# Step 0's ScalarE order, both copies of its transposed rows on VectorE, and an earlier k load in a planned attention-and-FFN kernel

## Chip, core and metric

The kernel runs on one core of a Trainium2 chip. Times are device microseconds of that core, the median of several executions. The profile is one execution taken by the hardware profiler; times in it count from the start of its span.

## What is computed

A gated linear attention over 768 positions feeds a gated feed-forward layer (ReGLU). Cut to what matters:

```python
# q, k, v, f_logit: (4, 8, 768, 48); w_gate, w_val: (384, 1536); w_out: (1536, 384)
f = 1.0 / (1.0 + np.exp(-f_logit))
for t in range(S):
    state = f[:, :, t, :, None] * state + np.einsum('bhd,bhe->bhde', k[:, :, t], v[:, :, t])
    y[:, :, t] = np.einsum('bhd,bhde->bhe', q[:, :, t], state)
x = y.transpose(0, 2, 1, 3).reshape(B * S, H * D)       # 3072 tokens x 384
out = (np.maximum(x @ w_gate, 0.0) * (x @ w_val)) @ w_out
```

## The kernel before

Time is cut into six steps (c = 0 to 5) of 128 positions, and each step works on the four batch entries as two pairs (pair 0 is b = 0, 1; pair 1 is b = 2, 3). A tile of one batch entry is 128 positions by 384 columns, 8 heads of 48.

For each pair, ScalarE forms exp(-f) (L563 in step 0, L649 in the others) and its log(1 + x) (L564, L651). TensorE sums that over the positions with a triangular matrix (`cum`, L572 or L658). ScalarE takes the exponentials of plus and minus the sum (L576 and L579 in step 0, L668 and L670 later), and k and q are multiplied by them into `hats` (L582, L584; L680, L683 on GpSimd). TensorE transposes `hats` (L609, L694), the result is copied out of PSUM into `qkT`, and then come the scores (L724), the mask (`ptm`, L734, VectorE), the weighted sum (`intra`, L759), the copy into `xT` (L788, ScalarE) and the state update (L810, L543, L547, L549). Small exponentials of the total decay go into `dec` (L598 in step 0, two per pair).

Step 0 differs from the other steps: `attention_pair` handles two batch entries at once, with two neighbouring positions in one partition. The copy of the transposed k (x = 1) is on VectorE (L617), and that of the transposed q (x = 0) on ScalarE (L616). An entry `tails["first q"]` makes the log of pair 1 (L564) come behind the q copy of pair 0 in ScalarE's order.

The feed-forward layer for the 512 tokens of a step has 12 hidden slices j of 128 (`ffn_hidden`): gate matmuls and value matmuls (L834), a ReLU on ScalarE (L840), a product on VectorE (L844); then the output matmuls (`ffn_out`, L877), a copy (L887) and a store (L891). In steps 0 to 2 the slices 0 to 5 are done for each pair apart, and slices 6 to 11 for all four together. All feed-forward matmuls form one fixed chain: gate 0, value 0, gate 1, and so on. The weights come in three slices each (`wg0` to `wg2`, `wv0` to `wv2`, `wo0` to `wo2`; slice 0 serves j = 0 to 3, slice 1 j = 4 to 7). They are issued by GpSimd, which also converts them to bf16 (L493). The inputs f, k, q, v are loaded by SyncE, one transfer per pair (L473, named f0.0, f0.1, f1.0 and so on: step, pair).

No order is written out by hand apart from the first loads. A class `Plan` takes every operation with a planned duration (`occ`), a latency and a priority, plays the schedule through, and so fixes the order of every engine, SyncE and GpSimd included. Each engine then runs its list strictly in that order and waits on semaphores where needed. `follows` adds an order without a wait; `after` adds a wait. The first loads are given by the string `first`; an item `x@y` is issued only when y has landed:

```python
first = ("f0.0 k0.0 q0.0 v0.0 f0.1 k0.1 q0.1 v0.1 wg0@f0.1 wv0 wg1@q0.1 wv1 wg2 wv2 f1.0@wv1 k1.0 q1.0 v1.0 wo0@q1.0 wo1 wo2 "
         "f1.1 k1.1 q1.1 v1.1").split()
```

The loads of SyncE keep the order of this list among themselves, and the weight transfers of GpSimd likewise. Up to about 15 us, TensorE's planned gaps are filled with matmuls on zeros (L938), which keep it busy and compute nothing.

Of the kernel before, what the change touches and what calls it, by code (L numbers as in the profile page):

```python
# [6 lines left out]
ALU = mybir.AluOpType  # L7
# [292 lines left out]
def bass_hgrn2_outer__then__ffn_reglu_kernel(  # L300
# [13 lines left out]
    x_way = {(c, pr): "tiled" if c < 3 else "xbar" for c in range(6) for pr in range(2)}  # L314
    s_twin = {(c, pr) for c in range(6) for pr in range(2)} - {(0, 0), (1, 0)}
    y_twin = {(1, 1), (2, 0), (2, 1)}
    flight = 3
    wsteps = 3
    first = ("f0.0 k0.0 q0.0 v0.0 f0.1 k0.1 q0.1 v0.1 wg0@f0.1 wv0 wg1@q0.1 wv1 wg2 wv2 f1.0@wv1 k1.0 q1.0 v1.0 wo0@q1.0 wo1 wo2 "
             "f1.1 k1.1 q1.1 v1.1").split()  # L320
    B, H, S, D = q.shape
    C = 128
    NC = S // C
# [66 lines left out]
    def act_t(n):  # L390
        return dict(occ=0.17 + n / 1150.0, lat=0.2)
# [63 lines left out]
    def slot_of(n, c, pr):  # L455
        return (2 * c + pr) % NL[n]

    def in_keys(n, c, b0, b1):
        return [f"{n}{slot_of(n, c, b // 2)}_{b % 2}" for b in range(b0, b1)]

    def load(n, c, b0, b1, after=()):
        last = tails.get("load")
        t = ld[n]
        both = c in twos and n != "v"
        if both:
            src = bass.AP(tensor=srcs[n].tensor, offset=b0 * H * S * D + c * C * D,
                          ap=[[2 * D, C // 2], [S * D, 2 * H], [1, 2 * D]])
            dst = bass.AP(tensor=t, offset=slot_of(n, c, b0 // 2) * 2 * HD, ap=[[NL[n] * 2 * HD, 128], [2 * D, H], [1, 2 * D]])
        else:
            src = bass.AP(tensor=srcs[n].tensor, offset=b0 * H * S * D + c * C * D,  # L470
                          ap=[[D, C], [S * D, (b1 - b0) * H], [1, D]])
            dst = t[:, slot_of(n, c, b0 // 2), :, :, :].rearrange("p b h d -> p (b h) d")
        op = add("SP", lambda: sy.dma_start(dst, src), [], in_keys(n, c, b0, b1),  # L473
                 occ=0.7 if both else 1.0, lat=0.9, prio=c * 100, after=after,
                 follows=[last] if last else [])
        tails["load"] = op
        dma(op, f"{n}{slot_of(n, c, b0 // 2)}", 0.95 * (b1 - b0), (64, 19, 27) if both else (128, 13.5, 23))
        return op

    WJ = NJ // wsteps  # L480
# [15 lines left out]
        dma(op, f"{nm}{s}", 2.45, (32, 62, 80, 2.2) if nm == "wo" else (24, 80, 80, 2.9))  # L496
        return op

    loads, done = [], {}
    for item in first:  # L500
        item, _, behind = item.partition("@")
        gate = [done[behind]] if behind else []
        if item[0] == "w":
            op = load_w(item[:2], int(item[2:]), gate)
        else:
            c, pr = (int(x) for x in item[1:].split("."))
            op = load(item[0], c, 2 * pr, 2 * pr + 2, gate)
        done[item] = op
        if item[0] != "w":
            loads.append(op)  # L510

# [40 lines left out]
    def attention_pair(c, b0):  # L552
# [9 lines left out]
        bkeys = [f"bn{bi}_0", f"bn{bi}_1"]  # L562
        add("ACT", lambda: sc.activation(raw["f"], raw["f"], AF.Exp, scale=-1.0), key["f"], key["f"], prio=P, **act_t(2 * HD))  # L563
        add("ACT", lambda: sc.activation(bn[:, :, :, 0:D], by_i["f"], AF.Ln, bias=1.0), key["f"] + [f"bneg{bi}"], bkeys, prio=P,  # L564
            follows=tails.pop("first q", []), **act_t(2 * HD))
        heads = lambda b_: b_.ap[:, 0:HD].rearrange("p (h d) -> p h d", h=H)
        for i in range(2):
            bc, ek = Bank("bc4"), Bank("bc4")

            def cum(i=i, bc=bc):  # L570
                for o in range(2):
                    mm = te.matmul(bc.ap[:, 0:HD], (upto if o <= i else below)[:, :], bn[:, o, :, 0:D], start=(o == 0), stop=(o == 1))  # L572
                return mm
            chain("cum", "PE", cum, ["upto", "below", f"bneg{bi}"] + bkeys, [bc], occ=0.33, lat=PE_L, prio=P + 1, opens=[bc])
            ex = expo[:, e0 + i, 0, :]
            add("ACT", lambda bc=bc, ek=ek: sc.activation(ek.ap[:, 0:HD], bc.ap[:, 0:HD], AF.Exp, scale=1.0),  # L576
                [bc], [ek], prio=P + 2 + i, opens=[ek], **act_t(HD))
            eqk = bc if i else f"expq{e0}_0"
            add("ACT", lambda bc=bc, i=i, ex=ex: sc.activation(bc.ap[:, 0:HD] if i else ex, bc.ap[:, 0:HD], AF.Exp, scale=-1.0),  # L579
                [bc], [eqk], prio=P + 2 + i, **act_t(HD))  # L580
            e, hi = ("DVE" if i else "POOL"), his[i]
            hk_op = add("DVE", lambda i=i, hi=hi, ek=ek: ve.tensor_tensor(hats[:, hi, 1, :, 0:D], by_i["k"][:, i], heads(ek), ALU.mult),  # L582
                        key["k"] + [ek, f"hats{hi}"], hk_(hi), prio=P + 2 + i, **dve_t(HD))
            add(e, lambda e=e, i=i, hi=hi, bc=bc, ex=ex: engine[e].tensor_tensor(  # L584
                hats[:, hi, 0, :, 0:D], by_i["q"][:, i], heads(bc) if i else ex.rearrange("p (h d) -> p h d", h=H), ALU.mult),
                key["q"] + [eqk, f"hats{hi}"], hq_(hi), prio=P + 3 + i, follows=[hk_op] if i else [], **elem_t(e, HD))
# [9 lines left out]
        for j in range(2):  # L596
            lo = 64 * j
            add("ACT", lambda lo=lo, j=j: sc.activation(  # L598
                dec[ai][lo:lo + 64, b0:b0 + 2, :, j].rearrange("p b n -> p n b"),
                tot.ap[lo:lo + 64, 0:2 * NP].rearrange("p (n b) -> p n b", n=NP), AF.Exp, scale=-1.0),  # L600
                [tot, f"dec{ai}"], [f"dec{ai}_{b}{j}{hh}" for b in (b0, b0 + 1) for hh in range(2)], prio=P + 10, **act_t(8))
        for x in (1, 0):
            tp = Bank("tp")

            def transposes(x=x, tp=tp):
# [6 lines left out]
            chain("transposes", "PE", transposes, ["ident"] + [t for hi in his for t in (hk_(hi) if x else hq_(hi))], [tp],  # L612
                  occ=0.5, lat=PE_L, prio=P + 4, opens=[tp])
            dst = bass.AP(tensor=qkT, offset=q0 * 2 * NP * C + x * 2 * NP * C, ap=[[NQ * 2 * NP * C, 128], [1, 2 * NP * C]])
            e = "DVE" if x else "ACT"
            op = add(e, (lambda tp=tp, dst=dst: sc.activation(dst, tp.ap[:, :].bitcast(BF16), AF.Copy)) if e == "ACT"  # L616
                else (lambda tp=tp, dst=dst: ve.tensor_copy(dst, tp.ap[:, :].bitcast(BF16))),  # L617
                [tp], [f"qkT{q0 + b}_{x}{hh}" for b in range(2) for hh in range(2)], prio=P + 4,
                occ=1.02 if e == "ACT" else 0.7, lat=0.2)
            if not x and b0 == 0:  # L620
                tails["first q"] = [op]

    def attention_back(c, b, behind):
        w = c * B + b
# [14 lines left out]
    def attention_front(c, b):  # L639
# [32 lines left out]
        if c < NC - 1:  # L672
            for j in range(2):
# [6 lines left out]
        add("POOL", lambda: gp.tensor_tensor(hk, kin[:, b % 2, :, :], ex[:, 1, :].rearrange("p (h d) -> p h d", h=H),  # L680
                                             ALU.mult),
            in_keys("k", c, b, b + 1) + [f"expk{ei}", f"hats{hi}"], hk_(hi), prio=P + 2, **pool_t(HD))
        add("POOL", lambda: gp.tensor_tensor(hq, qin[:, b % 2, :, :], ex[:, 0, :].rearrange("p (h d) -> p h d", h=H),  # L683
                                             ALU.mult),
            in_keys("q", c, b, b + 1) + [f"expq{ei // 2 * 2}_{ei % 2}", f"hats{hi}"], hq_(hi), prio=P + 2, **pool_t(HD))

        if (c, b // 2) in pe_hats:
            tp = Bank("tp")
# [203 lines left out]
                     occ=0.35 * len(both), lat=0.9, prio=P)  # L892
            dma(op, f"osb{oi}", 0.6, (8, 66, 66), len(both))

    groups = {c: [(0, 2, range(0, n)), (2, 4, range(0, n)), (0, 4, range(n, NJ))] for c, n in halves.items()}
    pend = []
    for c in range(NC):
        for b in range(0, B, 2):
# [32 lines left out]
    for e in pl.ENGINES:  # L931
        pl.free0[e] = 0.8
    spare = banks[-1]
    order = pl.settle([(bk, warm_until if bk is spare else 0.0) for bk in banks], rounds=8, early=set(done.values()))
    waits = pl.needs()

    def warm():
# [91 lines left out]
```

## Time and profile before

| | |
|---|---|
| median of 5 runs | 196.06 us (193.85 to 198.23) |
| the profiled execution | 198.23 us; its span 196.5 us |
| TensorE busy, with the filling matmuls | 185.4 us (94% of the span) |
| ScalarE, VectorE, GpSimd busy | 110.9, 106.2, 75.9 us |
| granted TensorE clock | 1.000 |
| moved by DMA | 31.74 MB, 162 GB/s over the span |

PE is TensorE's matmuls, PEld its weight loads, DVE VectorE, ACT ScalarE, POOL GpSimd, SPq and POOLq the queues of SyncE and GpSimd. A row of the timeline has the start, the length, the engine, the line, the operation with what it writes and reads, and in brackets how long the engine had been idle and what ended that. A row of the table of stretches has the stretch, its length, and the busy time of each engine in it.

### The profile page before, as it was taken

What the parts mean: (1) busy time and instruction counts of PE and PEld (TensorE: products, weight loads), DVE (VectorE), ACT (ScalarE), POOL (GpSimd) and SP (SyncE); (2) the same over time, 40 slices, a digit from 0 to 9 for tenths busy, and PEclk for the clock granted to TensorE, in tenths of its full rate; (3) what the DMA queues carried; (4) which work ended last, traced back from release to release, by engine and by line L of the source; (5) the groups of instructions that cost most, each with busy time, mean ns of one, the idle gap of its engine ahead of it and who ended that gap; (6) DMA issues with size and microseconds to landing.
All of it is one profiled execution on the core that took longest, in us unless ns stands there. A gap on an engine that the chain in (4) does not pass through costs nothing.

```text
span 196.5 us, 4465 instructions
## 1 busy us (share of the span) xinstructions
PE 185.4 (94%) x1790; PEld 110.6 (56%) x1790; DVE 106.2 (54%) x195; ACT 110.9 (56%) x250; POOL 75.9 (39%) x108
## 2 busy tenths in 40 slices
PE   6976899998999999999979979999999999999995
PEld 1445594455778556767744635554554555544564
DVE  7756884771577888354756733742554633442300
ACT  3676449662496879828656757378344433344312
POOL 8367003956375949772623183543230000000000
PEclk9999999999999999999999999999999999999999
DMA  5999999998998999999788897997974110111113
GB/s 136 275 277 206 206 188 214 195 204 170 233 243 176 223 185 178 229 180 232 161 178 151 169 232 148 243 220 160 213 91 99 60 48 16 40 40 43 40 40 120
DMA packets 118196, 31.74 MB, mean 162 GB/s; under 512 B 111136, under 2 KB 118176, under 8 KB 118176
## 3 DMA queue, kind: packets, MB, share of 16 engines
q1 hardware_dynamic: 114192, 27.93, 68.5%
q0 software_dynamic: 3984, 3.54, 11.3%
q8 instruction: 14, 0.23, 0.5%
q14 instruction: 6, 0.05, 0.1%
HBM read 25.95 MB, written 4.72 MB: 156 GB/s over the span
## 4 chain that ended last, share of the span: by engine, by line
PE 64%; DMA 13%; issue 8%; POOL 7%; SPq 5%; ACT 2%; POOLq 0%
PE ps L834 33%; PE ps L877 21%; DMA wo<-in_moe_w_out_dram 5%; SPq L473 4%; DMA k_in<-in_k_dram 3%; DMA q_in<-in_q_dram 3%; DMA f_in<-in_f_logit_dram 3%; PE ps L724 2%; POOL hats L680 2%; POOL hats L683 1%; PE ps L694 1%; PE ps L759 1%; PE ps L658 1%; SPq L795 1%; PE ps L810 1%
## 5 line engine op out<-in xcount | busy, mean ns | idle before, releaser
L844 DVE TENSOR_TENSOR gT<-relu,ps 128x512 bf16<-128x512 bf16 (+1 forms) x90 | 51.3, 578 | 54.0 <-PE ps L834 38.8
L834 PE MATMUL ps<-xT,wv 128*128 128x512 bf16 (+1 forms) x270 | 61.5, 337 | 1.5 <-DMA wv<-in_moe_w_val_dram 1.5
L834 PE MATMUL ps<-xT,wg 128*128 128x512 bf16 (+1 forms) x270 | 61.5, 337 | 0.2 <-ACT relu L840 0.2
L840 ACT ACTIVATE relu<-ps 128x512 bf16<-128x512 f32 (+1 forms) x90 | 45.3, 511 | 27.7 <-PE ps L834 27.2
L877 PE MATMUL ps<-wo,gT 128*128 128x384 bf16 x276 | 49.5, 326 | 0.7 <-DMA wo<-in_moe_w_out_dram 0.7
L877 PEld LDWEIGHTS ps<-wo,gT 128*128 128x128 bf16 x276 | 25.9, 98 | 18.0 <-DMA wo<-in_moe_w_out_dram 1.1
L834 PEld LDWEIGHTS ps<-xT,wv 128*128 128x128 bf16 x270 | 24.6, 98 | 19.6 <-DMA wv<-in_moe_w_val_dram 1.9
L834 PEld LDWEIGHTS ps<-xT,wg 128*128 128x128 bf16 x270 | 25.1, 98 | 17.8 <-ACT relu L840 0.3
L734 DVE TENSOR_TENSOR ptm<-ps,tri 128x512 bf16<-128x512 f32 x48 | 30.5, 684 | 8.6 <-PE ps L724 8.5
L680 POOL TENSOR_TENSOR hats<-k_in,expo 128x384 bf16<-128x384 f32 x20 | 19.8, 997 | 22.0 <-DMA k_in<-in_k_dram 12.1
L887 ACT ACTIVATE osb<-ps 128x384 f32<-128x384 f32 x23 | 11.3, 489 | 27.6 <-PE ps L877 27.4
L683 POOL TENSOR_TENSOR hats<-q_in,expo 128x384 bf16<-128x384 f32 x20 | 19.7, 998 | 5.6 <-DMA q_in<-in_q_dram 5.6
L549 POOL TENSOR_TENSOR st<-ssum,dec 128x384 bf16<-128x384 f32 x16 | 13.3, 829 | 15.8 <-DVE ssum L547 15.8
L649 ACT ACTIVATE f_in<-f_in 128x768 f32<-128x768 f32 x10 | 8.4, 843 | 13.2 <-DMA f_in<-in_f_logit_dram 13.2
L714 POOL CAST vpad<-v_in 128x384 bf16<-128x384 f32 x24 | 11.7, 504 | 4.3 <-DMA v_in<-in_v_dram 4.3
L547 DVE TENSOR_TENSOR ssum<-ps,st 128x384 f32<-128x384 f32 x16 | 8.8, 552 | 6.5 <-PE ps L810 6.5
L668 ACT ACTIVATE expo<-ps 128x384 f32<-128x384 f32 x20 | 9.9, 493 | 0.5 <-PE ps L661 0.3
L699 DVE COPY qkT<-ps 128x1024 bf16<-128x1024 bf16 x8 | 5.5, 690 | 8.5 <-PE ps L694 8.4
L670 ACT ACTIVATE expo<-ps 128x384 f32<-128x384 f32 x20 | 9.9, 496 | 0.0
L810 PE MATMUL ps<-vpad,hats 128*128 128x96 bf16 x80 | 6.7, 206 | 2.3 <-POOL vpad L714 2.3
L724 PEld LDWEIGHTS ps<-qkT 48*128 48x128 bf16 x192 | 5.4, 94 | 5.5 <-issue 2.0
L724 PE MATMUL ps<-qkT 48*128 48x128 bf16 x192 | 7.6, 217 | 0.9 <-ACT qkT L616 0.7
(76 smaller groups left out, 147.8 us busy)
## 6 DMA issues: line engine op xcount, KB each, us to landing
f_in<-in_f_logit_dram SPq DMA_DIRECT2D x12, 384.0 KB, 5.6
k_in<-in_k_dram SPq DMA_DIRECT2D x12, 384.0 KB, 5.1
q_in<-in_q_dram SPq DMA_DIRECT2D x12, 384.0 KB, 5.7
v_in<-in_v_dram SPq DMA_DIRECT2D x12, 384.0 KB, 5.4
out_dram<-osb SPq DMA_DIRECT2D x23, 192.0 KB, 2.3
wg<-in_moe_w_gate_dram POOLq DMA_DIRECT2D x3, 384.0 KB, 7.8
wv<-in_moe_w_val_dram POOLq DMA_DIRECT2D x3, 384.0 KB, 9.0
wo<-in_moe_w_out_dram POOLq DMA_DIRECT2D x3, 384.0 KB, 7.5
```

What stands on the lines that cost most here:

```text
L549: add("POOL", lambda: gp.tensor_tensor(t4(s_new), t4(tmp), rate, ALU.mult), [key] + dk, [f"S{b}_{c % 2}"], prio=P + 8, **pool_t(HD))
L668: add("ACT", lambda: sc.activation(ex[:, 1, :], bc.ap[:, 0:HD], AF.Exp, scale=1.0), [bc], [f"expk{ei}"], prio=P + 1, **act_t(HD))
L680: add("POOL", lambda: gp.tensor_tensor(hk, kin[:, b % 2, :, :], ex[:, 1, :].rearrange("p (h d) -> p h d", h=H), ALU.mult), in_keys("k", c, ...
L683: add("POOL", lambda: gp.tensor_tensor(hq, qin[:, b % 2, :, :], ex[:, 0, :].rearrange("p (h d) -> p h d", h=H), ALU.mult), in_keys("q", c, ...
L714: add("POOL", lambda vin=vin, vout=vout: gp.tensor_copy(vout, vin.rearrange("p (n j) d -> p n j d", j=2)), in_keys("v", c, b, b + 1) + [f" ...
L724: mm = te.matmul(s[j].ap[:, p * C:(p + 1) * C], tokens(c, b, 1, p, lo, lo + D), tokens(c, b, 0, p, lo, lo + D))
L734: add("DVE", lambda mi=mi, j=j, s=s: ve.tensor_tensor(ptm[mi][:, j, :, :], s.ap[:, :].rearrange("p (n t) -> p n t", n=NP), mask, ALU.mult) ...
L834: mm = te.matmul(bank.ap[:, 0:n], wt[:, kt, j * 128:(j + 1) * 128], xT[xi][:, kt, n0:n1], start=(kt == 0), stop=(kt == NK - 1))
L840: add("ACT", lambda: sc.activation(relu[ri][:, 0:n], gate.ap[:, 0:n], AF.Relu), [gate], [f"relu{ri}"], prio=P, **act_t(n))
L844: add("DVE", lambda: ve.tensor_tensor(gT[gi][:, j, n0:n1], relu[ri][:, 0:n], val.ap[:, 0:n], ALU.mult), [val, f"relu{ri}"], [f"gT{gi}_{j}_ ...
L877: mm = te.matmul(o[b].ap[:, 0:DM], gT[gi][:, j, b * C:(b + 1) * C], wo[:, j, :], start=(j == 0), stop=(j == NJ - 1))
L887: add("ACT", lambda b=b, oi=oi: sc.activation(osb[oi][:, :], o[b].ap[:, 0:DM], AF.Copy), [o[b]], [f"osb{oi}"], prio=P, **act_t(DM))
```

## The change

Four things are changed; the rest of the diff adds options that stay at their neutral setting (`act_copies`, `dve_q` and `single` are empty sets).

1. In step 0, the two `dec` exponentials of a pair are ordered behind the last exponential for q of that pair (`follows=[eq_op]`).
2. In step 0, the q copy goes to VectorE like the k copy.
3. The order "log of pair 1 behind the q copy of pair 0" is dropped.
4. In the list of first loads, k1.0 stands ahead of f1.0 and is released by the landing of wg1; f1.0 is still released by wv1. And k1.1 is now released by the landing of wo0, where it had no release of its own.

```diff
-    first = ("f0.0 k0.0 q0.0 v0.0 f0.1 k0.1 q0.1 v0.1 wg0@f0.1 wv0 wg1@q0.1 wv1 wg2 wv2 f1.0@wv1 k1.0 q1.0 v1.0 wo0@q1.0 wo1 wo2 "
-             "f1.1 k1.1 q1.1 v1.1").split()
+    act_copies, dve_q, single = set(), set(), set()
+    first = ('f0.0 k0.0 q0.0 v0.0 f0.1 k0.1 q0.1 v0.1 wg0@f0.1 wv0 wg1@q0.1 wv1 wg2 wv2 k1.0@wg1 f1.0@wv1 q1.0 v1.0 wo0@q1.0 wo1 wo2 f1.1 k1.1@wo0 q1.1 v1.1').split()
...
         add("ACT", lambda: sc.activation(bn[:, :, :, 0:D], by_i["f"], AF.Ln, bias=1.0), key["f"] + [f"bneg{bi}"], bkeys, prio=P,
-            follows=tails.pop("first q", []), **act_t(2 * HD))
+            **act_t(2 * HD))
...
-            add("ACT", lambda bc=bc, i=i, ex=ex: sc.activation(bc.ap[:, 0:HD] if i else ex, bc.ap[:, 0:HD], AF.Exp, scale=-1.0),
+            eq_op = add("ACT", lambda bc=bc, i=i, ex=ex: sc.activation(bc.ap[:, 0:HD] if i else ex, bc.ap[:, 0:HD], AF.Exp, scale=-1.0),
...
-                [tot, f"dec{ai}"], [f"dec{ai}_{b}{j}{hh}" for b in (b0, b0 + 1) for hh in range(2)], prio=P + 10, **act_t(8))
+                [tot, f"dec{ai}"], [f"dec{ai}_{b}{j}{hh}" for b in (b0, b0 + 1) for hh in range(2)], prio=P + 10,
+                follows=[eq_op], **act_t(8))
...
-            e = "DVE" if x else "ACT"
-            op = add(e, (lambda tp=tp, dst=dst: sc.activation(dst, tp.ap[:, :].bitcast(BF16), AF.Copy)) if e == "ACT"
+            e = "ACT" if (x, pr) in act_copies else "DVE"
+            add(e, (lambda tp=tp, dst=dst: sc.activation(dst, tp.ap[:, :].bitcast(BF16), AF.Copy)) if e == "ACT"
...
-            if not x and b0 == 0:
-                tails["first q"] = [op]
```

## The prediction

> **What bounds the kernel now.** I read the busy shares first, then the table of stretches of 4 us, then the timeline of 4 to 47 us, the landings of the single transfers, and the chain of waits.
>
> TensorE carries 94% of the span, so a change counts only where it takes idle time from TensorE or adds some:
>
> ```profile
> PE 185.4 (94%) x1790; PEld 110.6 (56%) x1790; DVE 106.2 (54%) x195; ACT 110.9 (56%) x250; POOL 75.9 (39%) x108
> ```
>
> The table of stretches says where that idle time is (stretch, length, PE busy first). Columns after PE are PEld, DVE, ACT and POOL:
>
> ```profile
> 16.00:20.00 4.00, 3.18 (x45) 2.65 (x47) 2.14 (x5) 2.38 (x5) 2.22 (x4) 1.00 1.24 206
> 20.00:24.00 4.00, 3.09 (x47) 2.17 (x41) 3.56 (x7) 1.54 (x5) 0.00 (x0) 1.00 1.24 206
> 44.00:48.00 4.00, 3.29 (x46) 1.89 (x45) 0.88 (x2) 1.22 (x3) 2.43 (x3) 1.00 0.80 159
> 100.00:104.00 4.00, 2.71 (x30) 1.60 (x29) 1.64 (x4) 1.58 (x3) 0.98 (x3) 1.00 1.24 236
> 116.00:120.00 4.00, 3.23 (x24) 1.92 (x25) 2.27 (x4) 2.06 (x3) 2.74 (x5) 1.00 0.77 166
> ```
>
> Idle: 0.82 + 0.91 = 1.73 us from 16 to 24, 0.71 at 44 to 48, 1.29 at 100 to 104, 0.77 at 116 to 120. From 120 us to the last matmuls every stretch is full. So a microsecond won early is a microsecond won at the end, unless a later wait takes it back.
>
> The timeline of step 0, what this change touches:
>
> ```profile
> 7.69 0.36 ACT L598 ACTIVATE dec<-ps 64x8 f32<-64x8 f32 x2
> 8.07 0.47 ACT L576 ACTIVATE ps<-ps 128x384 f32<-128x384 f32 x1
> 10.48 0.84 ACT L563 ACTIVATE f_in<-f_in 128x768 f32<-128x768 f32 x1 [1.55 <-DMA f_in<-in_f_logit_dram]
> 11.23 1.00 ACT L616 ACTIVATE qkT<-ps 128x1024 bf16<-128x1024 bf16 x1
> 12.13 0.83 ACT L564 ACTIVATE bneg<-f_in 128x768 bf16<-128x768 f32 x1
> 12.29 0.63 PE L724 MATMUL ps<-qkT 48*128 48x128 bf16 x16 [0.72 <-ACT qkT L616]
> 16.86 0.69 DVE L617 COPY qkT<-ps 128x1024 bf16<-128x1024 bf16 x1 [0.25 <-PE ps L609]
> 17.63 1.02 ACT L616 ACTIVATE qkT<-ps 128x1024 bf16<-128x1024 bf16 x1
> 18.21 0.50 PE L834 MATMUL ps<-xT,wv 128*128 128x256 bf16 x3 [0.62 <-DMA wv<-in_moe_w_val_dram]
> 22.96 0.50 PE L834 MATMUL ps<-xT,wv 128*128 128x256 bf16 x3 [0.91 <-DMA wv<-in_moe_w_val_dram]
> ```
>
> The reader should see three things. ScalarE stands idle for f0.1 just before the q copy, then starts the exponential first, so the copy is late. The scores wait for that copy. And the feed-forward chain waits for the value weights at 18.21 and at 22.96: no faster attention moves those two moments. It can only put attention matmuls into the idle time before 22.96.
>
> The transfers around step 1:
>
> ```profile
> 22.93 0.37 SPq L473 DMA_DIRECT2D f_in<-in_f_logit_dram  x1
> 23.35 3.33 SPq L473 DMA_DIRECT2D k_in<-in_k_dram  x1
> 32.28 1.67 SPq L473 DMA_DIRECT2D k_in<-in_k_dram  x1
> 32.89 0.78 POOL L493 DMA_DIRECT2D wo<-in_moe_w_out_dram  x1 [14.66 <-DMA q_in<-in_q_dram]
> 46.25 3.42 PE L877 MATMUL ps<-wo,gT 128*128 128x384 bf16 x20 [0.70 <-DMA wo<-in_moe_w_out_dram]
> ```
>
> Landings (issue plus time to landing): wg1 at 13.18 + 7.8 = 21.0, wv1 at 22.95, f1.0 at 29.0, k1.0 at 30.3, q1.0 at 32.6, f1.1 at 35.8, k1.1 at 42.9, q1.1 at 47.3; wo0 at 39.9, wo1 at 43.5, wo2 at 46.2. The last of these is what TensorE waits for at 46.25.
>
> **What the Trainium skill says.** "PSUM — Partial Sum Buffer", section "Engine vs sequencer instructions": the queues of ScalarE, VectorE and GpSimd are strict first-in-first-out, and matmuls run in program order. The trace agrees: the copy at 11.23 stands behind the exponential that waited 1.55 us. "VectorE: DVE Perf Modes", section "Why PSUM operands drop a tier", caps a copy of bf16 from PSUM at two elements a cycle. From 1024 elements and the page's 0.96 GHz an estimate is 533 ns; the trace has 690 ns on VectorE (and 1000 to 1020 on ScalarE), and I use the trace. "DMA: Bandwidth & Descriptors", section "Queues, rings and completion order": each DMA engine takes turns between the queues that have work, packet by packet. The trace agrees in kind: k1.1 and q1.1, beside wo1 and wo2, took 10.6 and 13.3 us from issue to landing, where q1.0 without them took 5.9. The section "Anatomy of one DMA" says that the wait for a semaphore happens on the issuing sequencer; so a released load holds all that is queued behind it on SyncE.
>
> **The change, part by part.**
>
> *The dec exponentials behind q's.* Two instructions of 0.36 us together leave the gap before 8.07. The second pair of exponentials, the hats and transposes of pair 0 move up 0.36. Nothing waits for `dec` before the state products at 26.1, so the later place costs nothing.
>
> *The q copy on VectorE.* The k copy ends at 9.85 + 0.69 = 10.54, now 10.18; the q copy follows it and ends at 10.87 instead of 11.23 + 1.00 = 12.23. Scores of pair 0: 1.36 us earlier, at about 10.9. ScalarE has no copy between exponential and log, so the log starts at 11.3 instead of 12.13; dropping the third ordering is what allows this, the exponential itself stays at 10.48 because f0.1 lands then. VectorE takes 2 x 0.69 = 1.4 us more. Its masks of pair 0 (2.48 us) begin at 11.4 instead of 12.73, the hats of pair 1 at 13.8 instead of 15.13, and their copies end near 15.5 + 2 x 0.69 = 16.9 instead of 18.65. So the scores of pair 1, at 19.63 before, can run in the wait for the value weights up to 18.21. Masks are then done near 20.1 instead of 22.78, and the last `intra` (0.41 at 24.05), the back transposes (0.84 and 0.39) and the state matmuls (4 x 0.17) can come before 22.96. That is 2.3 us of matmuls, against 1.73 us of idle time. I take 1.5; the bounds are 0.5, if the plan leaves them behind value slice 4, and 1.7.
>
> *k1.0 ahead of f1.0.* k1.0 is issued at 21.0 instead of 23.35. Its data cannot slow wv1: transfers of SyncE take at least 3.8 us to land in this trace, and wv1 lands 1.95 us after this issue. It shares with wg2 and wv2, which are first needed near 33 us and landed at 24.8 and 26.7, so even 2 us more is covered. f1.0 keeps its issue at 22.95 but stands behind k1.0. Free of weights, loads land 1.5 to 1.7 us apart (q1.0 32.6, v1.0 34.3, f1.1 35.8); f1.0 can be late by one such distance at most, 30.7, or gain nothing from below, 29.0. I take 30. The sums and exponentials (29.06 to 32.7 before) then end at 33.6, as the hats began at 33.68; covered by the wait for q1.0. Where that cover is gone, 0.2 to 0.9 us of idle TensorE near 35.7. What k1.0 gained lets q1.0 be issued some 2 us earlier; it lands between 30.6 and 32.6, I take 31.5. This is an estimate from those issues.
>
> *k1.1 behind wo0.* A wait is added. Behind it on SyncE stand q1.1, v1.1 and f2.0. wo0 goes out with q1.0's landing, at 31.5, and took 7.0 us before; with only v1.0 and f1.1 beside it I take 6.5, so 38.0. k1.1 is issued then instead of 32.28, and lands at 38.0 + 5.1 (the median of k) = 43.1 against 42.9; q1.1 1.6 to 3 later, 44.7 to 46.1 against 47.3. The hats of pair 1 started at 43.81 and 47.33. wo1 and wo2 have the engines nearly to themselves from 34 to 40: I expect them at 40.5 and 42.5 instead of 43.5 and 46.2. The 0.71 us of waiting at 45.5 goes; what is late next is q1.1, with no price while it lands by 47.3.
>
> Sum: -1.5 (step 0) - 0.7 (wo2) = -2.2 us. On the profiled execution that is 198.23 - 2.2 = 196.0, a span of 194.3. That execution lies 2.17 above the median; the median goes from 196.06 to 193.9, a gain of 1.1%. What the planner does with the order after 50 us cannot be read from the diff; the waits there (1.29 + 0.77) can go or double, so plus or minus 2 us.
>
> **The rivals.**
>
> *Given back later.* TensorE arrives at 100 us about 2 us earlier, but the state matmuls there wait for a v load (the transfer was issued at 98.44 behind stores and transposes of SyncE), and those at 116.77 again. If these land no earlier, the idle time grows by what was won: 195.9. For it: the chain of waits runs through SyncE from 95.8 to 99. Against it: there SyncE itself waits for ScalarE's relu and copies, which come earlier too.
>
> *Slower: the wait for wo0 comes due late.* If q1.0 does not move, wo0 is issued at 32.9 and lands at 39.9; with the longest time of a weight slice (10.2) at 43.1. k1.1 needs 5.1 more, and q1.1 4.4 more, its distance before when wo1 and wo2 ran beside it: 49.4 to 52.6 instead of 47.3. The transposes at 49.5 began 0.2 after the last q hat, so TensorE would stand still there for 2.1 to 5.3 us. I take 3.0: 199.1. It decides from a landing of wo0 at about 38.5 on. Against it: the engines are freer than before while SyncE waits.
>
> *More than expected.* The new order also removes the two late waits, 2 us more: 191.9. Nothing in the trace speaks for it except that they hang on the order.
>
> **How the numbers follow.** Forecast 0.40 (193.9, its own range 192.6 to 195.2), given back 0.20, slower 0.30, more 0.10. A measurement of this kernel tells about 1% from no change. Faster by over 1%: 0.28 of the forecast's 0.40 and all of the 0.10, so 0.38. Within 1%: 0.12 + 0.20 + 0.02 of the slower case = 0.34. Slower: 0.28. The range 191.0 to 199.6 leaves out the upper part of the slow case (0.14) and 0.03 below.
>
> **What would show it.** Right: scores of pair 0 near 10.9, pair 1 before 18.2, 16 to 24 us with at most 0.4 us idle, wo2 landed by 43, no wait of L877 for wo. Wrong: idle time before L694 or the scores of step 1, k1.1 issued after 39, ScalarE waiting for f1.0 past 30.7, or more than 2 us of waiting for v at 100 to 120.

## The result, and the profile after

The changed kernel is slightly slower. Its median is 196.97 us (195.4 to 198.41), that of the kernel before on the same chip 195.98 us (193.83 to 198.23); the ratio is 1.0064, with a 95% interval of 1.0047 to 1.0080. The forecast was a gain of 1.1%. The profiled execution took 196.71 us with a span of 195.0 us. Ratios here leave out single runs that lie more than 1.5% above the fastest of their kernel; where that matters, the mean over all runs stands beside them (here 1.0048).

The busy shares first. TensorE is as full as before, and VectorE and ScalarE have exchanged about 1 us:

```profile
PE 185.0 (95%) x1788; PEld 111.0 (57%) x1788; DVE 107.6 (55%) x197; ACT 109.9 (56%) x248; POOL 75.9 (39%) x108
```

The table of stretches of the changed kernel, with the same five rows as before and two more (92 to 100):

```profile
16.00:20.00 4.00, 2.10 (x29) 1.49 (x28) 1.80 (x3) 0.47 (x2) 2.05 (x4) 1.00 1.24 206
20.00:24.00 4.00, 4.00 (x74) 3.04 (x69) 3.48 (x8) 2.20 (x6) 0.00 (x0) 1.00 1.24 206
44.00:48.00 4.00, 4.00 (x56) 2.54 (x55) 1.03 (x2) 1.47 (x3) 3.71 (x4) 1.00 1.24 238
92.00:96.00 4.00, 3.62 (x34) 3.00 (x31) 2.78 (x7) 2.53 (x9) 2.00 (x3) 1.00 1.12 143
96.00:100.00 4.00, 3.34 (x40) 1.93 (x41) 2.84 (x6) 1.23 (x3) 0.00 (x0) 1.00 1.02 204
100.00:104.00 4.00, 4.00 (x50) 2.29 (x49) 3.19 (x6) 2.03 (x4) 2.61 (x4) 1.00 1.03 202
116.00:120.00 4.00, 4.00 (x27) 2.22 (x25) 1.61 (x3) 3.00 (x7) 0.90 (x2) 1.00 0.95 200
```

From 16 to 24 TensorE idles 1.90 us, where 1.73 were idle before: step 0 won nothing. At 44 to 48 the idle time is gone, as forecast. The two late waits that I had read at 100 and 116 are gone too, but new ones stand at 92 to 100 (0.38 + 0.66) and, in rows not shown, at 104 to 116 (1.07 in all).

The timeline of step 0:

```profile
7.33 0.47 ACT L580 ACTIVATE ps<-ps 128x384 f32<-128x384 f32 x1 [0.92 <-PE ps L576]
7.71 0.49 ACT L583 ACTIVATE expo<-ps 128x384 f32<-128x384 f32 x1
8.23 0.47 ACT L580 ACTIVATE ps<-ps 128x384 f32<-128x384 f32 x1
8.99 0.36 ACT L602 ACTIVATE dec<-ps 64x8 f32<-64x8 f32 x2
10.33 1.29 DVE L622 COPY qkT<-ps 128x1024 bf16<-128x1024 bf16 x2 [0.57 <-PE ps L614]
11.68 0.63 PE L727 MATMUL ps<-qkT 48*128 48x128 bf16 x16 [0.29 <-DVE qkT L622]
17.25 0.69 DVE L622 COPY qkT<-ps 128x1024 bf16<-128x1024 bf16 x1 [0.32 <-PE ps L614]
19.04 0.50 PE L837 MATMUL ps<-xT,wv 128*128 128x256 bf16 x3 [1.83 <-DMA wv<-in_moe_w_val_dram]
19.81 0.63 PE L727 MATMUL ps<-qkT 48*128 48x128 bf16 x16
```

Both copies are on VectorE, and the scores of pair 0 start at 11.68 instead of 12.29. The last copy of pair 1 ends at 17.94. But its scores (19.81) still stand behind the first value matmul, which waits for its weights until 19.04, where it started at 18.21 before.

The transfers around step 1:

```profile
20.70 0.37 SPq L473 DMA_DIRECT2D k_in<-in_k_dram  x1
22.59 3.10 SPq L473 DMA_DIRECT2D f_in<-in_f_logit_dram  x1
32.57 2.26 POOL L494 DMA_DIRECT2D wo<-in_moe_w_out_dram  x3 [14.53 <-DMA q_in<-in_q_dram]
38.38 0.37 SPq L473 DMA_DIRECT2D k_in<-in_k_dram  x1
L880 PE MATMUL ps<-wo,gT 128*128 128x384 bf16 x276 | 49.8, 326 | 0.0
```

k1.0 went out at 20.70 and k1.1 at 38.38 (forecast 21.0 and 38.0). The slices of wo landed at 38.4, 40.3 and 43.1 (forecast 38.0, 40.5, 42.5). The last line, from the groups of instructions, has 0.0 us of idle time before the output matmuls. The slower rival, a late wo0 that leaves TensorE without q1.1, did not occur.

The row of GpSimd holds something that the forecast did not have. It issued the three slices of wo in a row, the last at 34.07. In the kernel before, the second and third stood behind two products and a cast:

```profile
36.03 1.54 POOL L493 DMA_DIRECT2D wo<-in_moe_w_out_dram  x2
```

There wo2 was issued at 36.82 and landed at 46.21, 9.4 us later; now it took 9.0. So 2.75 of the 3.1 us that it landed earlier come from its new place in GpSimd's list.

### The profile page after: what moved, and what is told of

Its sections match the earlier page's. It is cut to its first block, busy times and chain, and to the rows that moved or that the text cites. A ratio compares the mean times of both kernels' runs of the same rounds, so it can differ in the third digit from the quotient of the medians.

```text
span 195.0 us, 4470 instructions
## 1 busy us (share of the span) xinstructions
PE 185.0 (95%) x1788; PEld 111.0 (57%) x1788; DVE 107.6 (55%) x197; ACT 109.9 (56%) x248; POOL 75.9 (39%) x108
## 4 chain that ended last, share of the span: by engine, by line
PE 61%; DMA 24%; SPq 7%; ACT 4%; POOL 2%; issue 1%
PE ps L837 34%; PE ps L880 18%; DMA q_in<-in_q_dram 6%; SPq L473 5%; DMA f_in<-in_f_logit_dram 5%; DMA wv<-in_moe_w_val_dram 5%; DMA k_in<-in_k_dram 3%; DMA wo<-in_moe_w_out_dram 3%; DMA xT<-xn 2%; SPq L705 2%; PE ps L727 2%; PE ps L661 1%; POOL hats L687 1%; PE ps L813 1%; PE ps L860 1%; PE ps L697 1%
## 5 line engine op out<-in xcount | busy, mean ns | idle before, releaser
L837 PEld LDWEIGHTS ps<-xT,wg 128*128 128x128 bf16 x270 | 25.5, 98 | 18.2 <-DMA xT<-xn 0.6
L727 PE MATMUL ps<-qkT 48*128 48x128 bf16 x192 | 7.6, 217 | 1.3 <-DMA qkT<-hats 1.0
L727 PEld LDWEIGHTS ps<-qkT 48*128 48x128 bf16 x192 | 5.4, 94 | 6.1 <-issue 3.1
L654 ACT ACTIVATE bneg<-f_in 128x768 bf16<-128x768 f32 x10 | 8.4, 837 | 0.1
```

The lines of the kernel that those rows point to most:

```text
L727: mm = te.matmul(s[j].ap[:, p * C:(p + 1) * C], tokens(c, b, 1, p, lo, lo + D), tokens(c, b, 0, p, lo, lo + D))
L837: mm = te.matmul(bank.ap[:, 0:n], wt[:, kt, j * 128:(j + 1) * 128], xT[xi][:, kt, n0:n1], start=(kt == 0), stop=(kt == NK - 1))
```

## The kernel before was not what one execution showed

The kernel before, unchanged, in another execution (`b_again`).

> The kernel before, unchanged, for a second profile, since the first was taken of an execution 2.2 us above the median. If that execution was long by chance of its transfers, this one ends some 1 to 3 us earlier, with fewer than 2.3 us of idle TensorE between 100 and 120 us; the idle time from 16 to 24 us and the wait for wo2 near 46 us should be there in both (1.5 to 2 us and 0.4 to 1 us). If the late waits belong to the order, they are there again.

It took 196.14 us. Its table of stretches:

```profile
44.00:48.00 4.00, 2.80 (x41) 1.60 (x42) 0.96 (x2) 0.49 (x1) 3.74 (x4) 1.00 1.27 228
100.00:104.00 4.00, 4.00 (x37) 2.23 (x36) 3.10 (x6) 2.84 (x6) 1.78 (x3) 1.00 1.11 206
116.00:120.00 4.00, 4.00 (x27) 2.25 (x26) 1.15 (x2) 2.76 (x7) 1.64 (x2) 1.00 0.79 152
```

The waits of 1.29 and 0.77 us that I read at 100 and 116 are not there. The execution I predicted from (198.23 us) was the longest one of the kernel before, 2.09 us above this one, and these waits of 2.06 us are about that difference. Here TensorE idled 0.02 us from 84 to 120 us, and in three kernels below that keep the old loads and their order (`step0_only`, `before_more_fill`, `before_less_fill`) 0.02, 0 and 0.81 us. So the kernel before usually has little there for the change to win. The wait for wo differs too: 0.71 us in the first execution, 1.57 here (1.20 of it in the row at 44), and none in two of the kernels below that keep the old loads. And the idle time from 16 to 24 us, on which the step 0 term of the forecast rests, was 1.73 us in the first execution and 0.71 here, where I had expected 1.5 to 2 again.

## Experiments

**Halves of the change.** In these expectations L is the theory that the loss comes in with the new list of loads and what follows from it, S that it comes from step 0. `step0_only` has parts 1 to 3 and the old list; `loads_only` has the new list and the old step 0; `no_wo_gate` is the changed kernel without the wait of k1.1.

```diff
 no_wo_gate:
-    ... f1.1 k1.1@wo0 q1.1 v1.1
+    ... f1.1 k1.1 q1.1 v1.1
```

> Only the changes in step 0 (dec behind q, both copies on VectorE, log not held behind the copy); the list of first loads as before. GpSimd and SyncE keep their order wholly, TensorE changes places only between 20 and 24 us. Theory L (the loss comes from the new list of loads and the order planned behind it): same as before, ratio 0.995 to 1.002, at most 0.5 us gained. Rival S (the loss comes from step 0: VectorE is now the late engine and the scores stand in the way of the feed-forward chain): 0.5 to 1.5 us slower, ratio 1.003 to 1.008. The prediction's own step 0 term: 1.5 us faster, 0.992.

> Only the new list of first loads (k1.0 ahead of f1.0 on wg1, k1.1 on wo0); step 0 as before. Theory L: as slow as the changed kernel, ratio 1.004 to 1.009, with the wait for wo2 at 46 us gone and more idle time on TensorE between 85 and 120 us. Rival S: 0.7 us faster than before, ratio 0.995 to 0.998.

> The changed kernel without the wait of k1.1 for wo0: k1.0 ahead of f1.0 and the step 0 changes stay. If the wait for wo0 is what costs (by itself or through the order planned behind it): back to the time before or better, ratio 0.996 to 1.001, with the wait for wo2 near 46 us back. If k1.0 ahead of f1.0 costs: stays at 1.004 or above.

| kernel | median, us | before, us | ratio, 95% interval |
|---|---|---|---|
| step0_only | 195.89 | 195.53 | 1.0013 (0.9991 to 1.0034) |
| loads_only | 195.94 | 195.53 | 1.0014 (0.9989 to 1.0038) |
| no_wo_gate | 196.69 | 195.53 | 1.0070 (1.0046 to 1.0095) |

Neither half is a gain; `step0_only` lies in the range of theory L, `loads_only` in that of neither theory. By the means over all runs they are 1.0023 and 1.0036, which add up to about the whole loss. But only the first is a clean half. The traces show SyncE and GpSimd of `step0_only` in the order of the kernel before throughout; `loads_only` has a later order of its own (after 60 us, 16 of SyncE's places hold another operation than in the changed kernel), and so has `no_wo_gate` (20 places from 77 us on). `no_wo_gate` is as slow as the changed kernel, so leaving out the wait of k1.1 is no help; what the wait costs alone it does not show.

It shows another thing. With k1.1 issued at 31.41, beside wo, wo2 landed at 43.79 and TensorE did not wait for wo, against my expectation. In all kernels with the new loads GpSimd issues the three slices in a row. So the wait of k1.1 was not needed to end the wait for wo.

**Step 0: why the value weights come later.** In the changed kernel TensorE waits 1.8 us for wv0, in the kernel before 0.6 for this slice. Each of 16 DMA engines reports its part of a slice. In the trace, 15 of them had finished wv0 by 18.0 us in the changed kernel and by 18.1 in the one before; the last one finished at 19.0 and 18.2. A packet of another queue lies in this time. First the kernel before, then the changed one, both from the DMA view of 16.5 to 18.1 us (packets, MB, share of 16 engines):

```profile
q0 software_dynamic: 336, 0.33, 123.8%
```

```profile
q0 software_dynamic: 325, 0.32, 120.5%
q8 instruction: 1, 0.02, 3.7%
```

It is one packet of 16 KB of instructions, 0.95 to 0.98 us long on one DMA engine. The Trainium skill's page "Runtime: NRT & Kernel Launch", section "Instruction fetch mechanics", has instructions refilled in blocks of 16 KiB, by a DMA queue of the sequencer's own, and calls the cost mostly hidden; the trace has 14 such packets in all. In the kernels of the table below it starts when TensorE has begun 128 to 133 pairs of weight load and matmul. The new step 0 comes to this place earlier, so there the packet comes ahead of the last part of wv0, and in the old one at about its end. From the packet and landing records of the traces:

| kernel | packet starts | 15th engine done | last engine done |
|---|---|---|---|
| before | 18.20 | 18.13 | 18.17 |
| b_again | 18.26 | 18.27 | 18.29 |
| loads_only | 17.81 | 18.16 | 18.25 |
| after | 16.93 | 18.01 | 19.00 |
| step0_only | 17.29 | 18.33 | 19.49 |
| no_wo_gate | 17.21 | 18.18 | 19.24 |
| a_again | 17.51 | 17.80 | 18.38 |

Theory I of the expectations is that this packet causes the late landing and with it the loss; W, that the wait for value weights with nothing to do in it costs the time; O, that the later order does. Two edits of the changed kernel try the first two: `after_less_fill` leaves out 11 of its 22 fill matmuls (the expectation says 12), so that the packet falls behind the value matmul; `after_scores_first` puts the scores of pair 1 ahead of the value matmul, and ties the order of all engines from 28 us on to that of the changed kernel.

```diff
 after_less_fill:
+    busy = [x for i, x in enumerate(busy) if i % 2 == 0 or i >= 24]
 after_scores_first:
...
+        if (c, b0, j) == (0, 0, 0):
+            tails["ffn"].follows.append(tails["scores", 0, 2])
```

> The changed kernel without 12 of its filling matmuls on zeros (every second one of the first 24), nothing else moved. Theory I (one DMA engine also carries TensorE's instructions; in the changed kernel that packet of 16 KB starts at 16.9 instead of 18.2 us, ahead of the last part of value slice 0, whose landing it holds up from 18.1 to 19.0): with fewer instructions ahead of it the packet starts after TensorE has got past the wait, so wv0 lands at about 18.1, the first value matmul starts there and not at 19.0, idle time from 16 to 24 us falls from 1.9 to about 1.0; the whole is 0 to 0.9 us faster than the changed kernel. If the late landing comes from something else, wv0 still lands at 19.0 or later.

> The changed kernel with the scores of pair 1 in step 0 ahead of value slice 0 on TensorE, and the order of all engines from 28 us on tied to that of the changed kernel. The prediction counted on this filling of the wait. If TensorE's place in line is what loses the step 0 gain: scores near 18.0, idle time from 16 to 24 us falls by 0.5 to 0.6 and the whole by up to 0.6 us against the changed kernel (ratio to before 1.003 to 1.006). If the idle time only moves to the wait for value slice 1 at 22.6, no gain.

`after_less_fill`: 195.94 us, 1.0009 (0.9984 to 1.0033). By the mean over all runs it is 1.0023. The packet moved to 20.73, but in the profiled execution wv0 landed at 18.92 nevertheless, since one engine had been 1.0 us behind from wg0 on (17.04 for 16.04): single late engines also come without this packet. `after_scores_first`: 195.44 us, 0.9989 (0.9955 to 1.0022); the scores ran at 18.56, in the wait, and the idle time shrank to 1.00 us in 16 to 20. That is 1.5 us less than the changed kernel, more than the 0.6 us that were expected of filling this wait.

The reverse test is `before_more_fill`: the first seven fill matmuls of the kernel before in two halves each, the same work with seven more pairs. And `before_less_fill` leaves out every second one of the 24 fills in the kernel before.

```diff
 before_more_fill:
+    def half():
+        return te.matmul(spare[:, 0:256], zeros[:, 0:128], zeros[:, 0:256], start=True, stop=True, skip_group_check=True)
+    busy = [(op, half) for op, _ in busy[:7] for _ in range(2)] + busy[7:]
```

> The kernel before with its first seven 512-wide fill matmuls each split into two of 256, so that TensorE's program has seven more instruction pairs ahead of the first value matmul and the same work. Theory of the instruction packet: the 16 KB packet starts at 16.3 to 17.2 us instead of 18.2 us, ahead of the last part of wv0, wv0 lands at 18.8 to 19.3 us instead of 18.2 us, idle at 16 to 20 us grows by 0.7 to 1.2 us, and the time by 0.3 to 0.6%. Rival (the late landing in the changed kernel comes from its loads or from chance): wv0 at 18.0 to 18.4 us and a time within 0.2%.

> The kernel before without every second of its first 24 fill matmuls. If fewer fills are a gain of their own (a fill that runs holds up the next real matmul[...]): 0.993 to 0.997. If they help only the changed kernel, by moving its instruction packet or its value product: 0.999 to 1.003.

`before_more_fill`: 195.10 us against 195.28, 1.0000 (0.9965 to 1.0035). The packet started at 17.72, ahead of the last part of wv0, and that part was 0.65 us behind the 15th engine, at 19.82. The 15th itself was a microsecond later than in `before` (19.17), so the packet would explain the smaller part of the delay. The time did not change, where theory I asked for 0.3 to 0.6% more. `before_less_fill`: 195.35 against 195.65, 0.9999 (0.996 to 1.0039); its packet did not move back (18.41), and its last engine was 0.54 us behind. So the packet is at most one reason for a later wv0, a later wv0 by itself does not make the loss, and fewer fills are no gain of their own. One way in which an early wait fails to reach the end is seen at 44 us: in `before_more_fill` TensorE idled 1.69 us at 16 to 20, but then found wo landed and did not idle at 44 to 48, where `b_again` idled 1.20.

**The later order.** The planner computes the order of all engines anew, and the new loads change it far beyond the loads: in the traces, 28 of SyncE's 97 places hold another operation, the last at 145 us, and on the other engines, too, operations change places. Two kernels exchange this. All engines' lists from 60 us on are tied to those of the other kernel, and everything ahead of that stays:

```diff
+    LATE = {"PE": "...", "ACT": "...", "DVE": "...", "POOL": "...", "SP": "..."}   # operation numbers in the other kernel's order
+    for late in LATE.values():
+        late = [pl.ops[int(i)] for i in late.split()]
+        for one, two in zip(late, late[1:]):
+            two.follows.append(one)
     order = pl.settle(...
```

> The changed kernel with the order of all five engines from 60 us on tied to that of the kernel before; all four changes stay, and SyncE and GpSimd differ from before only in the changed loads and in six places up to 58 us. Theory O (the gain from the loads is there at 52 us, and the new order planned behind it loses it, and more, between 85 and 120 us): faster than the changed kernel by 1 us or more, ratio to before 0.992 to 1.001, idle TensorE from 84 to 120 us about as in the kernel before (0 to 1 us in most executions). Rival W (the time is lost before 60 us): stays at 1.004 to 1.008.

> The kernel before with the order of all five engines from 60 us on tied to that of the changed kernel; none of the four changes. Theory O: slower than before, ratio 1.004 to 1.012, with 1 us or more of idle TensorE between 84 and 120 us on waits for transposed tiles or v. Rival W: same as before, 0.998 to 1.002.

`after_late_before`: 195.11 against 195.81 us, 0.9987 (0.9962 to 1.0013). That is 0.77% or 1.5 us less than the changed kernel, with its step 0 and its loads untouched. By the mean over all runs it is 0.9970. `before_late_after`: 195.99, 1.0021 (0.9996 to 1.0045), short of the 1.004 to 1.012 expected and not told from nothing. So giving the changed kernel the old later order takes the loss away, but giving the kernel before the new one is not shown to bring it.

Where the time goes is seen in TensorE's waits from 84 to 120 us, first of the changed kernel, then of another execution of it (`a_again`, below), then of `after_late_before`:

```profile
PE ps L727 <- DMA qkT<-hats: 1.0, 1, 1.0
PE ps L813 <- POOL vpad L717: 0.6, 1, 0.6
PE ps L837 <- DMA xT<-xn: 0.5, 1, 0.5
```

```profile
PE ps L727 <- DMA qkT<-hats: 0.8, 1, 0.8
PE ps L661 <- ACT bneg L654: 0.6, 1, 0.6
```

```profile
PE ps L813 <- POOL vpad L717: 0.4, 1, 0.4
```

The wait of the scores (L727) for transposed rows comes in both executions of the changed kernel, though not in `after_less_fill` and `after_scores_first`, which have the same later order. The timeline of SyncE's queue shows how it comes about. The changed kernel, with the last product of GpSimd that the rows need in the first line:

```profile
84.86 1.00 POOL L687 TENSOR_TENSOR hats<-q_in,expo 128x384 bf16<-128x384 f32 x1
86.48 2.01 SPq L705 DMA_TRANSPOSE qkT<-hats  x1
88.54 0.58 SPq L473 DMA_DIRECT2D q_in<-in_q_dram  x1
89.16 1.52 SPq L894 DMA_DIRECT2D out_dram<-osb  x1
90.73 1.19 SPq L798 DMA_TRANSPOSE xT<-xn  x1
91.96 1.31 SPq L705 DMA_TRANSPOSE qkT<-hats  x1
96.66 0.62 PE L727 MATMUL ps<-qkT 48*128 48x128 bf16 x16 [1.04 <-DMA qkT<-hats]
```

`after_late_before`:

```profile
84.24 1.46 SPq L705 DMA_TRANSPOSE qkT<-hats  x1
87.39 2.57 SPq L705 DMA_TRANSPOSE qkT<-hats  x1
94.57 0.62 PE L727 MATMUL ps<-qkT 48*128 48x128 bf16 x16
```

GpSimd was done at 85.86, but the second transpose went out only at 91.96: it stood behind a load, a store and another transpose, and the store and that transpose waited for ScalarE. What SyncE waited for from 84 to 97 us in the changed kernel:

```profile
SPq L798 <- ACT relu L843: 1.8, 1, 1.8
SPq L894 <- ACT dec L678: 1.8, 2, 1.3
SPq L798 <- ACT osb L890: 1.1, 1, 1.1
```

In the old order the second transpose follows at 87.39, and the scores run at 94.57 without waiting.

The start of the n-th of 270 value matmuls (their order is fixed) shows gain and loss in whole executions. Old order here means that of the kernel before; executions whose trace lacks some of these matmuls are left out.

| kernel | 108th | 180th | 270th | 108th to 180th |
|---|---|---|---|---|
| before (the long execution) | 76.63 | 123.06 | 185.95 | 46.43 |
| b_again (old order) | 77.19 | 120.96 | 183.84 | 43.77 |
| before_more_fill (old order) | 77.53 | 121.23 | 184.12 | 43.70 |
| before_less_fill (old order) | 76.07 | 120.76 | 183.65 | 44.69 |
| step0_only (old order on SyncE and GpSimd) | 75.73 | 119.50 | 182.38 | 43.77 |
| loads_late_before (old order, below) | 75.46 | 119.34 | 182.22 | 43.88 |
| combo (old order, below) | 75.31 | 120.77 | 183.66 | 45.46 |
| after (new order) | 75.45 | 122.18 | 184.41 | 46.73 |
| a_again (new order) | 76.02 | 121.94 | 184.17 | 45.92 |
| no_wo_gate (an order of its own) | 76.92 | 122.51 | 184.74 | 45.59 |

The changed kernel is 1.2 to 1.7 us ahead of `b_again` at its 108th and 1.0 to 1.2 behind at its 180th. The new order moves 0.65 us of other matmuls ahead of that point (the rest takes 62.23 instead of 62.88 us), so what is lost is 1.5 us or more. But `combo` and the first execution of `before` lose as much there with the old order. TensorE's idle time from 84 to 120 us was 0.5 to 2.4 us in the five executions with the new later order on all engines (1.6 on average), and 0 to 2.45 us in nine with the old one (0.65 on average): a difference in the mean, with a wide spread in each.

**The change once more, and both repairs.** `a_again` is the changed kernel itself. `combo` has the scores first and the later order of before; `loads_late_before` is `loads_only` with the later order of before.

> The changed kernel itself, beside the next three on the same chip. If it is truly slower by the first comparison's size: 1.004 to 1.008 of the kernel before, about 197.0 us. If the first comparison's 0.6% was chance and the five edits that brought it back to 0.999 to 1.001 did nothing: 0.998 to 1.002. Profile: the value slice wv0 lands at 18.9 to 19.1 us and TensorE idles 1.5 to 2.0 us at 16 to 20 us if the instruction packet is the cause of the late landing; idle 1.5 to 2.5 us at 84 to 120 us if the later order is.

> The changed kernel with both repairs: the scores of heads 2 and 3 of step 0 ahead of the value product, and the order of all engines from 60 us on tied to that of the kernel before. If both losses are real and add: 0.4% less than either repair alone, 0.992 to 0.996, 194.3 to 195.1 us, idle below 1.2 us at 16 to 24 us and below 0.8 us at 84 to 120 us. If each repair only removes the same chance loss: 0.998 to 1.001.

> The kernel before with the new list of loads alone, and the order of all engines from 60 us on tied to that of the kernel before. If the loads gain 1 to 2 us by 50 us and the new order afterwards gives it back: 0.992 to 0.996, 194.3 to 195.1 us, with idle below 0.8 us at 84 to 120 us. If the loads gain nothing that lasts: 0.999 to 1.003.

| kernel | median, us | before, us | ratio, 95% interval |
|---|---|---|---|
| a_again | 196.24 | 195.28 | 1.0064 (1.0035 to 1.0092) |
| combo | 195.15 | 195.28 | 1.0002 (0.9971 to 1.0033) |
| loads_late_before | 194.82 | 195.28 | 0.9993 (0.9968 to 1.0019) |

The loss is real. The granted clock does not explain it: among executions with the same mean granted clock of 0.991, ten of `a_again` took 196.42 us on average and 31 of the kernel before 195.19. Nor does a late wv0 by itself: in the profiled execution of `a_again`, 196.46 us long, it landed at 18.38, 0.6 us earlier than in `after`, and TensorE idled 1.16 us at 16 to 20, not the 1.5 to 2.0 that theory I asked for. With the old later order, the loads gain little or nothing (between -0.3% and +0.2%): my expectation of 0.992 to 0.996 was wrong. And two repairs bring no more than one. `combo` also missed its idle times: 1.46 us at 16 to 24 and 1.52 at 84 to 120, where below 1.2 and 0.8 were expected.

**Which engines' order?** `after_queues_before` has SyncE and GpSimd from 60 us on in the order of before and the other engines in that of the changed kernel; `after_compute_before` is the mirror. `late_before_less_fill` is `after_late_before` without every second fill.

> The changed kernel with the order of SyncE and GpSimd from 60 us on tied to that of the kernel before, TensorE, ScalarE and VectorE tied to the changed kernel's own. If the loss is in the order of transfers and of GpSimd's copies (the waits for qkT, vpad and xT at 92 to 116 us): 0.998 to 1.001 and idle below 1 us at 84 to 120 us. If it is in the order of the computing engines: 1.004 to 1.008 and idle of 1.4 to 2.5 us there.

> The mirror: the changed kernel with the order of TensorE, ScalarE and VectorE from 60 us on tied to that of the kernel before, SyncE and GpSimd to the changed kernel's own. If the loss is in the order of SyncE and GpSimd: 1.004 to 1.008, idle of 1.4 to 2.5 us at 84 to 120 us. If it is in the computing engines: 0.998 to 1.001 and idle below 1 us. If either order fits only with its own partner: both of these kernels slower than 1.004.

> The changed kernel with the order of all engines from 60 us on as before, and without every second of its first 24 fill matmuls. If the late order costs about 0.7% and the fills about 0.5%, each by itself: 0.992 to 0.996, 194.0 to 194.9 us. If the repairs don't add, as two others didn't: 0.998 to 1.001.

| kernel | median, us | before, us | ratio, 95% interval |
|---|---|---|---|
| after_queues_before | 199.22 | 195.65 | 1.0147 (1.0097 to 1.0196) |
| after_compute_before | 196.46 | 195.65 | 1.0048 (1.0019 to 1.0077) |
| late_before_less_fill | 195.30 | 195.65 | 0.9979 (0.9947 to 1.0011) |

Each half of the old order alone is slower than the kernel before (the first in only six executions); only the whole is not. TensorE's waits from 80 to 120 us, first `after_queues_before`, then `after_compute_before` (an execution of 198.01 us, 1.5 above its kernel's median):

```profile
PE ps L813 <- POOL vpad L717: 2.5, 3, 1.0
PE ps L727 <- DMA qkT<-hats: 0.8, 1, 0.8
```

```profile
PE ps L727 <- ACT relu L843: 1.0, 1, 1.0
PE ps L661 <- ACT bneg L654: 0.2, 1, 0.2
```

With GpSimd in an order made for other matmuls, its casts of v come late three times. The wait for transposed rows (0.8) is there with SyncE's old order, and not with its new one. So the two do not point to one misplaced transfer of SyncE. That the loss lies in how the lists of the engines fit each other agrees with both results, and was the third case of the expectation; the late transpose is the part of it that both profiles of the changed kernel show.

**A version that beats both?** `late_before_less_fill` has the lowest ratio, and its interval still reaches 1.0011. Against the changed kernel it wins about 0.8%, against the kernel before nothing that is certain; by the means over all runs it and `after_late_before` are at 0.9972 and 0.9970.

**What stays open.** The new later order is not enough for the loss. `after_less_fill` and `after_scores_first` keep it on all engines and are yet not clearly slower than before (1.0009 and 0.9989), and `before_late_after` has it at 1.0021. Three different edits of the changed kernel, one of the later order and two of step 0, each take away much or all of the loss, and together no more. As far as these runs show, the loss needs the changed start and the new later order together; how the one acts through the other is not shown. The profile of `after_less_fill` has 2.4 us of idle time at 84 to 120, as much as the changed kernel, so the profile does not explain its time. That the packet makes wv0 late was seen together, not shown: a kernel with the packet alone taken out was not tried.

## Why the prediction was wrong

*The base.* The profile was read as if its waits belonged to the kernel. 2.06 us of them, at 100 and 116, belonged to one long execution. They were not in the sum, but they made "given back later" and "more than expected" look like questions of those two waits, and hid that `b_again` runs from 84 to 120 us with 0.02 us of idle time, where a new order has nothing to win. The second of them was also misread: v had landed at 115.42, and its cast stood behind the products for `hats` in GpSimd's list until 116.21. The 1.73 us of the step 0 term were in the sum, and a second execution had 0.71.

*Step 0, -1.5 us: the step that failed first.* The `dec` exponentials went behind, the copies to VectorE, as said. But of 1.36 us for pair 0 only 0.61 came. The sums ahead of it took 0.50, 0.53 and 0.62 us where they had taken 0.34, 0.33 and 0.49 before, and the first exponential started 0.40 later (7.33 for 6.93). The new place of `dec` gave 0.23 us and not 0.36: the exponentials of the two sums now start 0.52 apart (7.71 and 8.23), where they started 0.75 apart before. The slower sums come and go (last section): they are also in `before_more_fill` and `before_less_fill`, and not in `b_again`. For pair 1 the copies ended at 17.94, not 16.9. Then it went below the term's lower bound: "if the plan leaves them behind value slice 4" was my worry for the last matmuls, and the plan left even the scores behind value slice 0. I took 1.5 from between 0.5 and 1.7 with nothing in the trace that fixed the order. The runs have nothing in place of the 1.5 us: `step0_only` is at 1.0013 (0.9991 to 1.0034). The forecast that "no faster attention moves those two moments" (18.21 and 22.96) failed as well: the first moved, to 19.04. `after_scores_first` put the scores into the wait, as I had forecast; with the late loss repaired as well (`combo`) it gave 1.0002, so the 1.5 us were not there to be had.

*k1.0 ahead of f1.0: right.* Issued at 20.70; f landed near 29.8 (forecast 30), without a stall. Only q1.0 came later than forecast, 32.3 for 31.5; its issue stood behind that of f1.0, which held SyncE for 3.10 us.

*k1.1 behind wo0, -0.7 us: right in its landings, by luck.* The wait of the output matmuls went, and wo landed within 0.6 us of the forecast. But I had it from engines left free by k1.1, with the issues of wo1 and wo2 where they were; they were issued 2.7 us earlier, which I had not seen, and `no_wo_gate`, with k1.1 beside them, had no wait for wo either. The size was no fixed one: with the old loads that wait was 0.7, 1.6, 0, 0, 0.6 and 0.3 us in six executions (before, `b_again`, `step0_only`, `before_more_fill`, `before_less_fill`, `before_late_after`), a mean of about 0.5. Where TensorE had idled more in step 0, it mostly waited less for wo, so a part of it only paid for earlier waits. What the two parts won together, with the later order as before, is 0.13% (`after_late_before`, -0.4 to +0.1%; 0.3% by the mean over all runs): 0.3 to 0.6 us instead of 2.2.

*The order after 50 us, "plus or minus 2 us": the step that turned no gain into a loss.* It was put at nothing in the sum, as noise around it. In the changed kernel, against the old later order, it was worth about +1.5 us (1.0064 against 0.9987), though not by itself ("What stays open"). The rival "given back later" had the right queue, SyncE, and came near in time (95.8 to 99 us, where it was 86 to 92), but it had the wrong transfer (a v load, where it was a transpose of q and k), and it allowed no more to be lost than had been won. Its argument against, that the waits of SyncE for ScalarE come earlier too, fails on a queue that has a new order: there those waits stood in front of the transpose. "Anatomy of one DMA" in the Trainium skill's page "DMA: Bandwidth & Descriptors", used in the prediction for k1.1, says what was needed here: a wait is served on the issuing sequencer. It is written for GpSimd's transfers; this trace agrees for SyncE, with 6.1 us from GpSimd's last product (85.86) to the issue (91.96).

*The slower rival* had its place at wo0 and q1.1. The landing of wo0 at 38.4 was just under its limit of 38.5. q1.1 landed at 46.0, within the 47.3 that had no price, and TensorE did not wait for it; `no_wo_gate`, without this wait, is at 1.007.

## What to carry to other kernels

Where a planner sets the order, an edit of the first 40 us also edits everything after: compare the order of every queue before pricing the edit, and tie the later order to the old one to see what the edit itself is worth. Read a second execution before a wait is put into a sum: the one of before held 2 us that another did not have. And if a wait is followed by another that ends on its own transfer, time saved at the first is not time saved at the end.

## What was not expected of the hardware

- This packet of 16 KB of instructions takes 0.95 to 0.98 us on one DMA engine. Where it started before 17.4 us, the last of 16 engines finished wv0 0.7 to 1.2 us behind the 15th (seven executions, among them `after`, `step0_only` and `combo`); at 17.5 and 17.7 it was 0.6 behind (`a_again`, `before_more_fill`), from 17.8 to 18.3 at most 0.12 (five executions, among them `before` and `b_again`). Against this stand `after_late_before` (17.68, 0.04 behind) and three without every second fill, with the packet later and the last engine 0.35 to 1.0 behind (`before_less_fill`, `late_before_less_fill`, `after_less_fill`). The packet and a late engine go together, then, but neither always nor only.
- The same matmuls of the first sums take 0.33 or 0.50 us each, from one execution to the next, at a granted clock of 1.00 in the table of stretches; fewer or smaller fills ahead of them (`before_less_fill`, `before_more_fill`) had the slower ones, but so had the changed kernel with the same nine fills as before, and `after_scores_first`, with these nine too, had the faster ones (0.33). The Trainium skill's page "TensorE: Matmul & The Clock Gate", section "What's actually happening", says that full speed comes after a busy window of some 3.4 us, and that this window runs freely and does not begin with the kernel; different starts of full speed fit that, though no run here shows the window itself.
